# Output product of the last six half blocks with seven products for eight, and attention chunks every two steps

## The chip, the cores and the metric

The kernel runs on one core of a Trainium2 chip. The metric is the device time of an execution in microseconds. Each number quoted as a time is the median of four to eleven executions. A span, from the first to the last instruction in a trace, is some 2 us less than the time of the same execution. Times in the text that have a start, such as 346.78, are us from the start of the span. TensorE is PE in the profile, VectorE is DVE, ScalarE is ACT, GpSimd is POOL, and SyncE, which issues most transfers, is SP.

## The reference

Linear attention with a decaying state feeds a two-layer network with the activation h - tanh(h). All is float32.

```python
batch, n_heads, seq, head_dim = (4, 8, 768, 64)
n_tokens, d_model, d_ff = (3072, 512, 2048)

for t in range(S):                       # attention, per batch and head
    state = gamma[None, :, None, None] * state + einsum('bhd,bhe->bhde', k[:, :, t], v[:, :, t])
    y[:, :, t] = scale * einsum('bhd,bhde->bhe', q[:, :, t], state)
x = y.transpose(0, 2, 1, 3).reshape(B * S, H * D)
h = x @ w_in                             # 3072 x 512 by 512 x 2048
g = h - np.tanh(h)
return g @ w_out                         # 3072 x 2048 by 2048 x 512
```

## The kernel before

The 3072 tokens are 12 half blocks of 256 tokens. One step takes one half block and 256 of the 2048 hidden columns: an up product (x by w_in into PSUM), the activation on ACT and VectorE, and, two steps later, a down product (g by w_out). There are 96 steps. Attention is computed in chunks of 128 tokens, which are laid between the steps, from step 9 on one chunk in three steps.

The down product of a step is eight blocks of 128x128 by 256 columns, issued as four matmuls of 512 columns:

```python
    def down(n, m2, j, first, last):
        if first:
            o_p[j] = bank("o", f"o_{n}_{m2}_{j}")
            keep_busy(o_p[j][:, :P])
        for i in range(2):
            nc.tensor.matmul(o_p[j], gT[n, m2][:, i, ts(j, P)], w2[:, 2 * m2 + i],
                             start=(first and i == 0), stop=(last and i == 1))
```

The scores of a chunk need its q and k with head dimension on the partitions. From chunk 8 on that is done by two transfers: ACT splits the words into halves, a write takes them to memory (`rows`), and a transposing read brings them back (`kqT`). `products` has two groups of matmuls, and only the second needs `kqT`:

```python
    def turn_by_dma(ci):
        apart = mid.tile([P, 2, 2, H * D], U16, tag="apart", bufs=1)   # cut
        for which in range(2):
            words = loaded[ci][which].rearrange("p h d -> p (h d)").bitcast(U16)
            nc.scalar.copy(out=apart[:, :, which],
                           in_=words.rearrange("p (n two) -> p two n", two=2))
        rows = dram.tile([P, 2, 2 * H * D], U16, tag="rows")           # cut
        nc.sync.dma_start(out=rows, in_=apart.rearrange("p two i n -> p two (i n)"))
        sides[ci] = mid.tile([P, 2, NP, P], F32, tag="kqT")            # cut
        nc.sync.dma_start_transpose(out=sides[ci]..., in_=rows...)     # cut

    def products(ci):
        kh, _, vh = loaded[ci]
        kT, qT = (sides[ci][:, i] for i in range(2))
        ...                       # cut: k by v, 32 records, no kqT needed
        ...                       # cut: kT by qT, 32 records, need kqT
```

The loop over the steps. The order in which it names the operations is the order of every engine's queue. `turn_by_dma` stands at the end of a step, behind the activation in ACT's queue; what it makes for chunk ci + 3 is used by `products` at the start of the next chunk's step:

```python
    with_chunk = {BEGUN + 3 * i + 1: FIRST - 3 + i for i in range(NCH - FIRST + 3)}
    ...
    for s in range(BEGUN, len(steps)):
        n, m2, first, last = steps[s]
        ci = with_chunk.get(s)
        if ci is not None:
            if ci + 3 < NCH:
                scale(ci + 3, 0, nc.gpsimd)
                scale(ci + 3, 1, nc.gpsimd)
            if ci >= FIRST:
                outputs_rest(ci)
                keep_x(ci)
            if FIRST <= ci + 2 < NCH:
                products(ci + 2)
                mask(ci + 2)
                state(ci + 2)
            load_chunk(ci + 4)
            if FIRST <= ci + 1 < NCH - 1:
                outputs(ci + 1)
                see(ci + 1)
        for i in with_weights.get(s, []):
            convert(i)
            load_weights(i + 3)
        for i in range(2):
            up(n, m2, i)
        ...                                   # cut
        shrink_begin(n, m2)                   # two ACT operations
        shrink_factors(n, m2)                 # three ACT operations
        shrink_multiply(n, m2)
        downs(LAG)                            # the down product of two steps ago
        shrink_end(n, m2)
        if ci is not None and ci + 3 < NCH:
            turn_by_dma(ci + 3)
```

## Time and profile before

| | before |
|---|---|
| time | 752.49 us (752.43 to 754.41) |
| span of the trace (of an execution of 753.87 us) | 752.1 us |
| TensorE busy | 99% |
| a plain step (up and down) | 6.88 us |
| a chunk of attention, added to a step | 2.24 us |
| waits of TensorE for a transpose | none |

The views and how they are read are in the prediction below. A line of a group or of the timeline has the source line, engine, operation, and output<-inputs. In the chain of waits a line is start, duration, engine, tile, source line and number of records. Each float32 matmul of the source makes two records.

### The profile page before, as it was taken

The page shows a single profiled execution, that of the slowest core. Times are in us where ns is not written, and L with a number is a line of the kernel's source. Part 1 is how long each engine was busy: PE and PEld are TensorE (multiplying, and loading weights), DVE is VectorE, ACT ScalarE, POOL GpSimd, SP SyncE. Part 2 cuts the span into 40 slices and gives each one's busy share as a digit, 9 for nine tenths or more (in the row PEclk, how much of TensorE's full clock was granted, in tenths as well). Part 3 has the DMA queues.
Part 4 walks back from the last instruction along what each step waited for, and adds up shares of the span by engine and source line. Part 5 has one row for each costly group of instructions (what it writes and reads, how often), then busy time and mean ns, then how long its engine had stood idle before and what let it go on. Part 6 is the DMA issues. An engine that isn't in the chain of part 4 may idle for free.

```text
span 752.1 us, 13885 instructions
## 1 busy us (share of the span) xinstructions
PE 740.9 (99%) x5502; PEld 509.9 (68%) x5502; DVE 518.0 (69%) x807; ACT 389.4 (52%) x727; POOL 126.9 (17%) x108
## 2 busy tenths in 40 slices
PE   8899999999999999999999999999999999999997
PEld 7786667666767676766676676666666666666775
DVE  4889989998898666656565656565665666656653
ACT  4567576667665546445545545444344434434442
POOL 0565445445444111100111100000000000000000
PEclk9999999999999999999999999999999999999999
DMA  9972436556553353343342421000000000000000
GB/s 196 234 182 74 127 89 172 158 158 153 156 128 84 99 155 107 67 96 93 91 99 71 98 58 56 29 1 1 29 0 1 28 1 0 29 0 1 28 2 28
DMA packets 125680, 59.76 MB, mean 79 GB/s; under 512 B 109872, under 2 KB 118576, under 8 KB 125616
## 3 DMA queue, kind: packets, MB, share of 16 engines
q1 hardware_dynamic: 125328, 58.67, 29.9%
q8 instruction: 43, 0.70, 0.4%
q10 hardware_dynamic: 288, 0.21, 0.1%
q14 instruction: 21, 0.17, 0.1%
HBM read 35.80 MB, written 14.68 MB: 67 GB/s over the span
## 4 chain that ended last, share of the span: by engine, by line
PE 96%; DMA 2%; DVE 1%; SPq 1%; ACT 0%; issue 0%; ACTq 0%; DVEq 0%
PE h L414 44%; PE o L462 42%; PE y L352 3%; PE o L470 2%; PE s L298 2%; PE s L304 1%; PE kqTp L212 1%; PE kqTp L250 1%; DMA raw<-in_moe_w_in_dram 1%; DMA k<-in_k_dram 1%; SPq L229 1%; DMA out_dram<-sum 0%; SPq L154 0%; DVE power L187 0%; DVE head L185 0%; DVE a L311 0%
## 5 line engine op out<-in xcount | busy, mean ns | idle before, releaser
L414 PE MATMUL h<-xT,w 128*128 128x256 f32 x1536 | 349.9, 381 | 0.0
L414 PEld LDWEIGHTS h<-xT,w 128*128 128x128 f32 x1536 | 289.7, 190 | 68.4 <-issue 31.8
L462 PE MATMUL o<-w,g 128*128 128x512 f32 x736 | 331.9, 593 | 0.0
L462 PEld LDWEIGHTS o<-w,g 128*128 128x128 f32 x736 | 139.4, 190 | 135.1 <-issue 128.4
L423 ACT ACTIVATE u<-h 128x512 f32<-128x512 f32 x96 | 57.3, 597 | 289.0 <-PE h L414 288.9
L439 DVE TENSOR_TENSOR th<-h,th 128x512 f32<-128x512 f32 x96 | 66.3, 690 | 176.0 <-ACT th L424 176.0
L453 DVE COPY_PREDICATED g<-large,th 128x512 f32<-128x512 int32 x96 | 71.8, 748 | 10.2 <-DVE g L452 0.5
L442 DVE SCALAR_TENSOR_TENSOR h<-q,h 128x512 f32<-128x512 f32 x96 | 66.8, 696 | 10.4 <-DVE h L440 0.5
L448 DVE SCALAR_TENSOR_TENSOR h<-q,h 128x512 f32<-128x512 f32 x96 | 66.6, 694 | 8.2
L431 ACT ACTIVATE q<-u,tab 128x512 f32<-128x512 f32 x96 | 69.4, 722 | 0.0
L432 ACT ACTIVATE q<-u,tab 128x512 f32<-128x512 f32 x96 | 69.1, 720 | 0.0
L433 ACT ACTIVATE large<-u,tab 128x512 f32<-128x512 f32 x96 | 68.8, 717 | 0.0
L452 DVE TENSOR_TENSOR g<-h,u 128x512 f32<-128x512 f32 x96 | 66.3, 691 | 3.3
L440 DVE SCALAR_TENSOR_TENSOR h<-u,h 128x512 f32<-128x512 f32 x96 | 65.8, 685 | 0.0
L236 POOL TENSOR_TENSOR q<-q,tab 128x512 f32<-128x512 f32 x22 | 24.3, 1104 | 198.4 <-DMA q<-in_q_dram 115.1
L424 ACT ACTIVATE th<-h 128x512 f32<-128x512 f32 x96 | 56.9, 592 | 0.0
L195 POOL TENSOR_TENSOR low<-low,power 128x512 f32<-128x512 f32 x30 | 38.5, 1282 | 103.1 <-DVE power L187 89.1
L199 POOL TENSOR_TENSOR w<-low,head 128x512 f32<-128x512 f32 x30 | 38.7, 1289 | 2.4
L352 PEld LDWEIGHTS y<-a,v 64*64 64x64 f32 x768 | 15.8, 134 | 16.7 <-ACT large L433 10.6
L236 POOL TENSOR_TENSOR v<-v,tab 128x512 f32<-128x512 f32 x22 | 26.5, 1207 | 0.1
L382 ACT COPY seen<-y 64x1 f32<-64x1 f32 x96 | 10.1, 153 | 28.2 <-PE y L352 27.8
L393 ACT COPY xT<-y 128x512 f32<-128x512 f32 x24 | 14.1, 587 | 17.0 <-PE y L352 17.0
(54 smaller groups left out, 412.8 us busy)
## 6 DMA issues: line engine op xcount, KB each, us to landing
rows<-apart SPq DMA_DIRECT2D x16, 512.0 KB, 2.8
k<-in_k_dram SPq DMA_DIRECT2D x24, 256.0 KB, 4.3
q<-in_q_dram SPq DMA_DIRECT2D x24, 256.0 KB, 4.9
v<-in_v_dram SPq DMA_DIRECT2D x24, 256.0 KB, 5.1
raw<-in_moe_w_out_dram SPq DMA_DIRECT2D x12, 512.0 KB, 3.6
out_dram<-sum SPq DMA_DIRECT2D x23, 256.0 KB, 2.1
raw<-in_moe_w_in_dram SPq DMA_DIRECT2D x14, 256.0 KB, 4.2
raw<-in_moe_w_in_dram SPq DMA_DIRECT2D x28, 128.0 KB, 3.9
```

Of the source, the lines that this page charges most:

```text
L414: nc.tensor.matmul(hp, w1[:, c, ts(2 * m2 + i, P)], xT[n // 2][:, c, ts(n % 2, TH)], start=(i == 0 and c == 0), stop=(c == NC - 1), skip_g ...
L423: nc.scalar.activation(u, hp, AF.Square)
L431: nc.scalar.activation(q0, u, AF.Square, bias=bias0)
L432: nc.scalar.activation(q1, u, AF.Square, bias=bias1, scale=math.sqrt(A))
L433: nc.scalar.activation(large, u, AF.Relu, bias=bias_m)
L439: nc.vector.tensor_tensor(th, hp, th, op=ALU.subtract)
L440: nc.vector.scalar_tensor_tensor(hp, in0=u, scalar=R, in1=hp, op0=ALU.subtract, op1=ALU.mult, reverse0=True)
L442: nc.vector.scalar_tensor_tensor(hp, in0=q0, scalar=C0, in1=hp, op0=ALU.add, op1=ALU.mult)
L448: nc.vector.scalar_tensor_tensor(hp, in0=q1, scalar=A * C1, in1=hp, op0=ALU.add, op1=ALU.mult)
L452: nc.vector.tensor_tensor(flat, hp, u, op=ALU.mult)
L453: nc.vector.copy_predicated(flat, large.bitcast(I32), th)
L462: nc.tensor.matmul(o_p[j], gT[n, m2][:, i, ts(j, P)], w2[:, 2 * m2 + i], start=(first and i == 0), stop=(last and i == 1))
```

## The change

The intent is to save one matmul in eight of the down product. Two blocks of tokens by two blocks of hidden columns are multiplied with two by two blocks of w_out by Strassen's algorithm (in a form with shared sums): seven products with sums of the left blocks on POOL in every step, sums of the weights made once on POOL, and seven sums of the results on VectorE at the end of each half block. That needs the buffers of the weights' conversion and of the chunks' q and k, and all PSUM banks that attention uses. So it can be done only when attention is over. For that the chunks are put in one step of two; attention then ends in step 45, and the last six half blocks (steps 48 to 95) run with seven products. Third, x holds the even tokens of a half block first, and the output rows are stored to match.

```diff
+        half = xT[n][:, :, ts(nj // 2, TH)].rearrange("p (n r) t -> p r n t", r=2)
+        y = y_banks[:, ci % 2][:, :: 1 - 2 * (ci % 2)]
+        for odd in range(2):
+            nc.scalar.copy(out=half[:, :, :, ds(P * odd + D * (nj % 2), D)],
+                           in_=y[:, :, :, odd::2])
...
+    def fast_sums(n, m2):
+        g = gT[n, m2]
+        a11, a12, a21, a22 = (g[:, i, ts(j, P)] for j in range(2) for i in range(2))
+        s_ = inp.tile([P, 4, P], F32, tag="kq"[m2 % 2], name=f"s_{n}_{m2}", bufs=2)
+        s1, s2, s3, s4 = (s_[:, i] for i in range(4))
+        nc.gpsimd.tensor_tensor(s1, a21, a22, op=ALU.add)
+        nc.gpsimd.tensor_tensor(s2, s1, a11, op=ALU.subtract)
+        nc.gpsimd.tensor_tensor(s3, a11, a21, op=ALU.subtract)
+        nc.gpsimd.tensor_tensor(s4, a12, s2, op=ALU.subtract)
+        fast_g[n, m2] = (a11, a12, s4, a22, s1, s2, s3)
...
+        five, sixth = spare
+        first, second, third = five[:3]
+        acc = {1: first, 2: first, 5: second, 7: second, 3: third, 4: third, 6: sixth}
...
+        for k in (1, 6, 5, 7, 4, 2, 3):
+            right = (
+                w2[:, 2 * m2, :TH], w2[:, 2 * m2 + 1, :TH], w2[:, 2 * m2 + 1, TH:],
+                *(t_of[x, m2 // 2][:, m2 % 2] for x in (3, 0, 1, 2)),
+            )[k - 1]
+            nc.tensor.matmul(accs[n][k], left[k - 1], right, start=first and k in (1, 6, 5, 4),
+                             stop=last, skip_group_check=True)
...
+        nc.scalar.copy(out=p1, in_=acc[1])
+        for dst, k, b, how in (
+            (v_, 6, p1, add), (x_, 5, v_, add), (w_, 7, v_, add), (c22, 5, w_, add),
+            (c21, 4, w_, sub), (c11, 2, p1, add), (c12, 3, x_, add),
+        ):                                    # one VectorE operation each
...
-    with_chunk = {BEGUN + 3 * i + 1: FIRST - 3 + i for i in range(NCH - FIRST + 3)}
+    with_chunk = {BEGUN + 2 * i + 1: FIRST - 3 + i for i in range(NCH - FIRST + 3)}
...
+        if n >= FAST:                         # FAST = 6
+            fast_sums(n, m2)
+        if s in with_fast:
+            fast_weights(*with_fast[s])
         if ci is not None and ci + 3 < NCH:
             turn_by_dma(ci + 3)
```

More of the change, by code (lines that the diff above doesn't have):

```diff
@@ L392, in keep_x @@
             xT[n] = xp.tile([P, NP, BLK * P], F32, tag="xT", name=f"xT_{n}")
-        nc.scalar.copy(
-            out=xT[n][:, :, ts(nj, P)].rearrange("p (n r) t -> p r n t", r=2),
-            in_=y_banks[:, ci % 2][:, :: 1 - 2 * (ci % 2)],
-        )
+        half = xT[n][:, :, ts(nj // 2, TH)].rearrange("p (n r) t -> p r n t", r=2)
[3 more added lines that the diff above has]
+                           in_=y[:, :, :, odd::2])
     gT = {}
@@ L463, in down @@
                              start=(first and i == 0), stop=(last and i == 1))
-    def down_half(n, m2, j, c, first, last):
-        if first and c == 0:
-            o_p[j] = banks("t", f"o_{n}_{m2}_{j}")
-        for i in range(2):
-            nc.tensor.matmul(o_p[j][:, c, :TH], gT[n, m2][:, i, ts(j, P)],
-                             w2[:, 2 * m2 + i, ts(c, TH)],
-                             start=(first and i == 0), stop=(last and i == 1))
-    def store_half(n, j, c):
-        o = sums[n][0][:, j]
-        at = out[ds(n * TH + j * P, P)]
-        if c == 0:
-            nc.scalar.copy(out=o[:, :TH], in_=o_p[j][:, c, :TH])
-            nc.sync.dma_start(out=at[:, :TH], in_=o[:, :TH])
-            return
-        for quarter, copy, queue in (
-            (2, nc.vector.tensor_copy, nc.sync),
-            (3, nc.scalar.copy, nc.scalar),
-        ):
-            cols = ts(quarter, P)
-            copy(out=o[:, cols], in_=o_p[j][:, c, ts(quarter - 2, P)])
-            queue.dma_start(out=at[:, cols], in_=o[:, cols])
     def add_up(n, m2, j):
@@ L501, in add_up, with rows_of @@
         if done:
-            nc.sync.dma_start(out=out[ds(n * TH + j * P, P)], in_=o)
+            nc.sync.dma_start(out=rows_of(n)[:, j], in_=o)
+    def rows_of(n):
+        return out[ds(n * TH, TH)].rearrange("(p two) c -> p two c", two=2)
     runs = []
@@ L516, with quarter, fast_weights @@
     steps = [(n, m2, i == 0, i == len(r) - 1) for r in runs for i, (n, m2) in enumerate(r)]
+    FAST = 6
+    PAIRS = NM // 2
+    room = []
+    t_of = {}
+    def quarter(i, c, at):
+        return w2[:, i::2, ts(c, TH)][:, ds(2 * at, 2)]
+    def fast_weights(k, at):
+        if not room:
+            for _ in range(3):
+                raw = stage.tile([P, 2, 2, TH], F32, tag="raw", name="fast_raw", bufs=3)
+                room.extend(raw[:, i] for i in range(2))
+            for tag in ("head", "low", "power"):
+                room.extend(stage.tile([P, 2, TH], F32, tag=tag, name=f"fast_{tag}")
+                            for _ in range(2))
+            late = xp.tile([P, 4, 2, TH], F32, tag="xT", name="fast_x")
+            room.extend(late[:, i] for i in range(4))
+        t = t_of[k, at] = room[PAIRS // 2 * k + at]
+        a, b = (
+            (quarter(0, 1, at), quarter(0, 0, at)),
+            (quarter(1, 1, at), t_of.get((0, at))),
+            (quarter(1, 1, at), quarter(0, 1, at)),
+            (t_of.get((1, at)), quarter(1, 0, at)),
+        )[k]
+        nc.gpsimd.tensor_tensor(t, a, b, op=ALU.subtract)
@@ new lines @@
+    fast_g = {}
+    def fast_sums(n, m2):
[8 more added lines that the diff above has]
+        fast_g[n, m2] = (a11, a12, s4, a22, s1, s2, s3)
@@ new lines, with fast_banks @@
+    spare = []
+    accs = {}
+    def fast_banks(n):
+        if not spare:
+            t = banks("t", "fast_t")
+            whole = y_banks.rearrange("p two r n t -> p r two n t")
+            spare.append([t[:, 0], t[:, 1], whole[:, 0].rearrange("p two n t -> p (two n t)"),
+                          bank("o", "fast_o"), bank("o", "fast_o")])
+            spare.append(whole[:, 1].rearrange("p two n t -> p (two n t)"))
+        five, sixth = spare
+        first, second, third = five[:3]
+        spare[0] = five[3:] + [first, second, third]
+        acc = {1: first, 2: first, 5: second, 7: second, 3: third, 4: third, 6: sixth}
+        right = {2: 1, 7: 1, 4: 1, 6: n % 2}
+        accs[n] = {k: b[:, ts(right.get(k, 0), TH)] for k, b in acc.items()}
@@ new lines, in fast_down @@
+    def fast_down(n, m2, first, last):
+        if first:
+            fast_banks(n)
+        left = fast_g.pop((n, m2))
+        for k in (1, 6, 5, 7, 4, 2, 3):
[5 more added lines that the diff above has]
+                             stop=last, skip_group_check=True)
@@ new lines, in fast_end @@
+    def fast_end(n):
+        acc = accs.pop(n)
+        o = op.tile([P, 2, DM], F32, tag="sum", name=f"sum_{n}")
+        c11, c12, c21, c22 = (o[:, j, ts(c, TH)] for j in range(2) for c in range(2))
+        some = [mid.tile([P, 2, TH], F32, tag="a", name=f"fast_{n}") for _ in range(2)]
+        p1, v_, x_, w_ = (t[:, i] for t in some for i in range(2))
+        nc.scalar.copy(out=p1, in_=acc[1])
+        add, sub = ALU.add, ALU.subtract
+        for dst, k, b, how in (
+            (v_, 6, p1, add), (x_, 5, v_, add), (w_, 7, v_, add), (c22, 5, w_, add),
+            (c21, 4, w_, sub), (c11, 2, p1, add), (c12, 3, x_, add),
+        ):
+            if how is sub:
+                nc.vector.tensor_tensor(dst, b, acc[k], op=sub)
+            else:
+                nc.vector.tensor_tensor(dst, acc[k], b, op=add)
+            if k == 4:
+                nc.sync.dma_start(out=rows_of(n)[:, 1], in_=o[:, 1])
+        nc.sync.dma_start(out=rows_of(n)[:, 0], in_=o[:, 0])
@@ L518 @@
     waiting = []
     def part(j, n, m2, first, last):
-        if n == 2 * NB - 1 and j == 1:
-            for c in range(2):
-                down_half(n, m2, j, c, first, last)
-                if last:
-                    store_half(n, j, c)
-            return
         down(n, m2, j, first, last)
@@ L533, in downs @@
             tile_ = waiting.pop(0)
+            if tile_[0] >= FAST:
+                fast_down(*tile_)
+                if tile_[3]:
+                    fast_end(tile_[0])
+                continue
             for j in range(2):
@@ L597 @@
         with_weights[i - 5] = [i]
+    with_fast = {4 * NM // 2 + 1 + i: (i % 4, i // 4) for i in range(2 * PAIRS)}
     for s in range(BEGUN, len(steps)):
```

## The prediction

> **What bounds the kernel now.** I read the page from the top: the busy shares and slices, then the chain that ended last.
>
> ```profile
> PE 740.9 (99%) x5502; PEld 509.9 (68%) x5502; DVE 518.0 (69%) x807; ACT 389.4 (52%) x727; POOL 126.9 (17%) x108
> PE   8899999999999999999999999999999999999997
> PE 96%; DMA 2%; DVE 1%; SPq 1%; ACT 0%; issue 0%; ACTq 0%; DVEq 0%
> ```
>
> TensorE is busy in every slice and is 96% of the chain. The time is a sum of matmuls, so a matmul less should be time less, as long as nothing makes TensorE wait. The groups, one kind of matmul each, say where that time sits:
>
> ```profile
> L414 PE MATMUL h<-xT,w 128*128 128x256 f32 x1536 | 349.9, 381 | 0.0
> L462 PE MATMUL o<-w,g 128*128 128x512 f32 x736 | 331.9, 593 | 0.0
> L423 ACT ACTIVATE u<-h 128x512 f32<-128x512 f32 x96 | 57.3, 597 | 289.0 <-PE h L414 288.9
> ```
>
> L414 is the first product (x by w_in), L462 the output product, the one that the change touches. Each float32 matmul of the source appears as two records: a step has 8 in the source on L414, and 1536 records are 16 for each of 96 steps. The means (381, 593 ns) overlap; what counts is the pace in the chain. ACT waits 289 us for L414: it follows TensorE.
>
> The chain in order of time, around one chunk of attention (a 128-token piece, now one in three steps), gives the pace:
>
> ```profile
> 422.26 0.39 PE y L352 x16
> 422.65 0.47 PE s L298 x32
> 423.12 0.47 PE s L304 x32
> 423.58 0.70 PE y L352 x47
> 424.28 3.65 PE h L414 x16
> 427.94 3.43 PE o L462 x8
> 431.37 3.45 PE h L414 x16
> 434.82 3.43 PE o L462 x8
> 438.25 3.45 PE h L414 x16
> 441.71 3.43 PE o L462 x8
> 445.14 0.39 PE y L352 x16
> ```
>
> A plain step is 3.45 + 3.43 = 6.88 us. Chunk to chunk is 445.14 - 422.26 = 22.88 us, so a chunk adds 22.88 - 3 x 6.88 = 2.24 us. There are no gaps.
>
> Lastly, the timeline around the step of another chunk, for what must happen between two chunks. A chunk's q and k are split into halves by ACT, written to memory (rows), and read back transposed (kqT); L304 of the next chunk needs kqT:
>
> ```profile
> 308.75 0.65 PE L304 MATMUL s<-kqT 64*64 64x64 f32 x32
> 313.79 0.60 ACT L423 ACTIVATE u<-h 128x512 f32<-128x512 f32 x1 [3.18 <-PE h L414]
> 316.60 1.04 ACT L273 COPY apart<-k 128x1024 uint16<-128x1024 uint16 x1
> 317.53 1.05 ACT L273 COPY apart<-q 128x1024 uint16<-128x1024 uint16 x1
> 318.60 0.36 SPq L276 DMA_DIRECT2D rows<-apart  x1
> 321.30 1.85 SPq L278 DMA_TRANSPOSE kqT<-rows  x1
> 331.64 0.65 PE L304 MATMUL s<-kqT 64*64 64x64 f32 x32
> ```
>
> The table of DMA issues has the last link:
>
> ```profile
> kqT<-rows SPq DMA_TRANSPOSE x16, 4.2
> ```
>
> The reader should see a loop: L304 of a chunk at 308.75, this step's up product, five ACT operations, two copies, a write, a transpose issued at 321.30 that lands 4.2 to 4.4 us later, at about 325.6. The next L304 is at 331.64: 6 us of slack, in a schedule of three steps per chunk.
>
> **What the Trainium skill says.** (1) "TensorE: Matmul & The Clock Gate", Step-by-step, says that weight loads are pulled ahead of matmuls in flight. The trace agrees for exactly the shape that the change uses: L414 has a new load of 190 ns for every 256-column record and still runs 16 in 3.45 us, 216 ns each. (2) "DMA: Bandwidth & Descriptors", Anatomy of one DMA, puts about 2 us on any transfer, mostly completion; its Rules section says that a DMA which reads what another wrote waits for the first one's completion before it is issued. The trace agrees: the rows landed 2.6 us after their issue, and the transpose was issued 0.1 us after that. The two latencies stand in series and don't shrink when chunks come closer. (3) "GPSIMD Engine Reference", Elementwise, has a two-input float32 operation at 1.96 times VectorE's time. Here such operations took 1040 to 1290 ns against 690, 1.5 to 1.9 times. (4) The TensorE page, clock gate, says that the clock falls after an idle window of about 3.4 us; the trace is at 0.998 and shows no such idle, so only a wait that long would matter.
>
> **The change, part by part.**
>
> *Seven products for eight.* A step's output product is 8 blocks of 128x128 by 256 columns. In blocks of 256 columns (L414, and L470 in the last half block at 8 records in 1.73 us) one costs 3.45/8 = 0.431 us. Seven cost 3.02 us against 3.43: 0.41 to 0.42 us a step. Six half blocks of 8 steps are 48 steps; I count 47 here, 0.42 x 47 = **-19.7 us**, and the last in the end below. Each of the seven has its own weights, a load of 190 ns beside 431, hidden as in L414.
>
> *Sums for the left side*, four of 128x128 a step on POOL. From 1.04 to 1.29 us for 512 columns I estimate 0.35 to 0.5 us each, at most 2 us a step, on an engine with nothing else by then. g is ready some 5.6 us after its up product ends (L453 of the last step ends at 743.3, that product's records at 737.7), and is used two output and two up products later, 2 x 3.02 + 2 x 3.45 = 12.9 us. Hidden, +0.
>
> *Weight sums*, 16 on POOL of some 1.2 us, in steps 33 to 48, before first use in step 50. Hidden.
>
> *Recombination*, seven VectorE operations of 128x256 on PSUM; the same shape took 0.41 to 0.43 us (L323, L327), so 2.9 us per half block in place of one copy of 0.69 on VectorE and one on ACT. VectorE's own work is six operations of about 0.7 us, 4.2 us of a 6.5 us step, so it catches up in the next step; the five rotating banks give an up product (3.45 us) of room. Hidden, +0.
>
> *The end.* Before, from the last output products (744.40) to the end (752.1) 7.7 us, with a 0.86 us wait inside. After: 3.02 of matmuls, perhaps 0.3 for the last POOL sums, about 0.9 for the last two VectorE operations, 2.1 for the store (its row's median), 1.0 as before from landing to the end: 7.3. About **-0.4 us**.
>
> *x in two copies*, half the size each (a 128x256 ACT copy took 0.37 us against 0.59 for 128x512): +0.15 us of ACT in its idle time. +0.
>
> *A chunk every two steps.* TensorE, VectorE and ACT do the same chunk work, only sooner, so by busy shares it costs nothing. But the loop above gets only 2 x 6.88 + 2.24 = 16.0 us. From the start of L304 to the landing of the next kqT, over all 15 pairs in the trace, the loop takes 16.6 to 17.35 us, mean 16.9 (the one shown: 325.6 - 308.75 = 16.85), plus 0.1 to start. The mean natural distance, (468.70 - 126.86)/15 - 6.88 = 15.9. So TensorE, which works in order, should stand at L304 for about 1.1 us in each of 15 chunks: 16 us. It is a true loop: the next u, copies and transpose start from where TensorE resumes, so the wait comes back each time. The first transposed chunk is worse: its transpose was issued at 119.41 and landed 4.3 us later at 123.7, while its L304, at 126.86 now, comes one step earlier, near 119.9: 3.8 us. Together **+20 us**, and with fewer collisions, at 0.8 us a chunk, +16.
>
> Sum: 752.5 - 19.7 - 0.4 + 16 to 20 = 748.4 to 752.4. I take **750 us**: the matmuls saved in the second half are spent waiting in the first.
>
> **The rivals.** *A: the loop fits and nobody waits.* Then 752.5 - 20.1 = 732 us, 2.7% faster. For it speaks that TensorE is 99% busy and DMA engines are half idle; against it, 15 of 15 loops are longer than 16.0 us. Faster by over 2% needs 737.4 or less, a wait of under 5 us in all, where I count 16 at the least. *B: the denser DMA stretches the loop further.* In steps 9 to 26 chunk loads, rows, transposes and weights share the queues, and rows took up to 3.9 us and transposes 4.6 there. One more microsecond in nine loops makes 759 us. Against it: SP issues in order, so chunk loads and transposes stay apart. *C: VectorE becomes the bound in those steps.* It is at 9 tenths in the early slices (six operations, weight conversion and sums come to nearly a step). But a chunk brings it about 1.5 us (0.68 + 0.41 + 0.42) and TensorE 2.24, so denser chunks don't raise the ratio; it would add a few microseconds. *D: POOL or the recombination holds the fast half.* If the sums took twice my estimate they would still fit the 12.9 us; a stall at each of six half blocks of 1 us would be 6 us.
>
> **Range and chances.** Savings are firm to 1 us, since every duration was measured in the same shape. The wait is 0.6 to 1.5 us in 15 loops plus 2 to 4 once, 11 to 26 us. That gives 743 to 759; I take **742 to 758**. Faster by over 2% needs rival A almost whole: 0.07. Slower by over 2% (767.5) needs B and D together: 0.03. Within 2%: 0.90.
>
> **What would show it.** In the changed trace: output steps of the last six half blocks at 3.02 us and pairs of steps at 6.47; a TensorE wait for the kqT transpose, missing before, in about 16 places of some 1 us, the first near 4; chunk to chunk 17.0 us and not 16.0; no wait for POOL or VectorE of note in the second half; attention ending some 104 us sooner (its last step is 45 and not 63: 18 steps of 6.88 us are 124, less the 20 of waits). The prediction is wrong if chunk to chunk is 16.0, if the transposes land sooner than 4.1 us, or if TensorE stands in the fast half.

## The result

The changed kernel takes 758.68 us (758.23 to 759.18, four runs) against 752.49 us. The ratio is 1.0077, with a 95% interval of 1.0062 to 1.0092: no gain and 0.8% slower. A ratio is taken over the fast runs of both kernels, and is not quite the ratio of the medians that are quoted.

The page of the changed kernel, busy shares and the chain by engine:

```profile
PE 726.8 (96%) x5758; PEld 560.8 (74%) x5758; DVE 532.0 (70%) x843; ACT 389.4 (51%) x749; POOL 230.8 (30%) x316
PE 70%; DMA 14%; DVE 6%; ACT 6%; issue 2%; SPq 1%; POOL 0%; DVEq 0%; ACTq 0%; POOLq 0%
```

TensorE has 14 us less to do, and only 70% of the chain is TensorE, which was 96%. DMA is now 14% of it. Who TensorE waited for stands in the view of waits (total us, times, longest):

```profile
PE s L308 <- DMA kqT<-rows: 16.7, 16, 3.5
```

That line did not exist before. The chain in order of time, from one chunk's score products to the next, shows the loop; where a "..." stands, the short pieces between are left out:

```profile
346.78 0.69 PE s L308 x32
...
348.17 3.67 PE h L420 x16
...
354.16 0.61 ACT large L439
354.77 1.89 ACT apart L277 x2
...
356.68 2.63 DMA rows<-apart
...
359.37 4.10 DMA kqT<-rows
...
363.51 0.69 PE s L308 x32
```

The chain now runs through up product, activation, copies, write and transpose back to the score products, and the down product (beside the activation) and the whole second step are not on it. From 346.78 to 363.51 it takes 16.73 us.

In the fast half the same view shows a step as planned. Seven products of 0.43 us stand between two up products, 452.74 - 446.26 = 6.48 us a step against 6.88, without a gap:

```profile
446.26 3.45 PE h L420 x16
449.72 0.43 PE fast_t L579 x2
...
452.74 3.45 PE h L420 x16
```

Two more things stand out. The first wait, in TensorE's timeline, with the idle time before an instruction in brackets:

```profile
119.43 0.69 PE L302 MATMUL s<-v,k 64*64 64x64 f32 x32
123.58 0.87 PE L308 MATMUL s<-kqT 64*64 64x64 f32 x32 [3.46 <-DMA kqT<-rows]
124.38 5.18 PE L420 MATMUL h<-xT,w 128*128 128x256 f32 x16
```

The up product behind it takes 5.11 us in the chain where 3.45 is normal. The view by stretches shows the clock. A line has the stretch, its length, the busy time of PE, PEld, DVE, ACT and POOL, and then the clock that TensorE was granted:

```profile
120.54:123.95 3.41, 0.37 (x24) 0.37 (x28) 3.14 (x5) 0.00 (x0) 3.33 (x3) 1.00 0.95 215
123.95:127.36 3.41, 3.41 (x31) 2.75 (x22) 3.24 (x7) 0.00 (x0) 1.67 (x2) 0.50 1.18 220
```

TensorE was busy for 0.37 us of the first 3.41, and then had half the clock for 3.41 us. That is a loss of 1.7 us, as much as the up product was late; from 127.36 us on the view has 1.00 again.

And the end, in the timeline of all engines:

```profile
750.30 0.59 PE L579 MATMUL y<-w,s 128*128 128x256 f32 x2
750.50 0.37 ACT L588 COPY fast<-fast_t 128x256 f32<-128x256 f32 x1 [6.38 <-PE fast_t L579]
751.00 0.42 DVE L597 TENSOR_TENSOR fast<-y,fast 128x256 f32<-128x256 f32 x1 [4.15 <-PE y L579]
...
753.26 0.41 DVE L597 TENSOR_TENSOR sum<-y,fast 128x256 f32<-128x256 f32 x1
```

All seven recombining operations run after the last matmul (750.30 + 0.59), one after another, to 753.67.

Where the time went, from the two traces. A wait is counted as the start of L308 less the start of L302, less the 0.47 us (0.52 in the first two chunks) that lies between them undisturbed; this includes the tail of the products ahead, which the idle time in brackets does not.

| stretch | before | changed | difference |
|---|---|---|---|
| start to the up product of step 6 | 85.09 | 85.07 | 0.0 |
| from there to the last up product (734.23, 737.72) | 649.14 | 652.65 | +3.5 |
| of which 45 steps of 6.885 now 6.477 | | | -18.4 |
| of which 16 waits for transposes: 3.6, 2.3, and fourteen of 0.7 to 1.3 | | | +19.6 |
| of which the slow up product, 5.11 and not 3.45 | | | +1.7 |
| of which left over | | | +0.6 |
| from the start of the last up product to the end | 17.87 | 18.98 | +1.1 |
| span | 752.1 | 756.7 | +4.6 |

The times differ by 6.2 and these spans by 4.6. The traced execution of the kernel before was a long one (753.87 us): in seven later executions its span was 750.8 us in the median (749.8 to 751.2), which is 1.3 us of it; the other 0.3 lies outside the spans. The first row is the same work in nearly all kernels here, and yet takes from 83.8 to 85.4 us in their thirteen traces. So up to 1.6 us between two executions can come from the start, and what follows goes by stretches of the traces more than by spans.

### The profile page after: what moved, and what is told of

Read it like the earlier page. It is cut to its first block, busy times and chain, and to the rows that moved or that the text cites. A ratio compares the mean times of both kernels' runs of the same rounds, so it can differ in the third digit from the quotient of the medians.

```text
span 756.7 us, 14749 instructions
## 1 busy us (share of the span) xinstructions
PE 726.8 (96%) x5758; PEld 560.8 (74%) x5758; DVE 532.0 (70%) x843; ACT 389.4 (51%) x749; POOL 230.8 (30%) x316
## 4 chain that ended last, share of the span: by engine, by line
PE 70%; DMA 14%; DVE 6%; ACT 6%; issue 2%; SPq 1%; POOL 0%; DVEq 0%; ACTq 0%; POOLq 0%
PE h L420 37%; PE o L468 9%; DMA kqT<-rows 8%; PE fast_t L579 7%; PE y L579 6%; PE fast_o L579 5%; DMA rows<-apart 5%; ACT apart L277 3%; PE y L356 2%; PE s L308 2%; ACT q L437 1%; ACT q L438 1%; ACT large L439 1%; ACT th L430 1%; PE kqTp L254 1%
## 5 line engine op out<-in xcount | busy, mean ns | idle before, releaser
L468 PE MATMUL o<-w,g 128*128 128x512 f32 x384 | 173.0, 593 | 0.0
L468 PEld LDWEIGHTS o<-w,g 128*128 128x128 f32 x384 | 72.6, 190 | 71.4 <-issue 68.4
L544 POOL TENSOR_TENSOR s<-g 128x128 f32<-128x128 f32 x48 | 21.9, 455 | 294.4 <-DVE g L459 214.1
L459 DVE COPY_PREDICATED g<-large,th 128x512 f32<-128x512 int32 x96 | 73.9, 770 | 9.5
L308 PE MATMUL s<-kqT 64*64 64x64 f32 x768 | 16.5, 223 | 16.7 <-DMA kqT<-rows 16.7
L579 PE MATMUL fast_t<-w,g 128*128 128x256 f32 x96 | 28.6, 380 | 0.0
```

Of the source, the lines that this page charges most:

```text
L459: nc.vector.copy_predicated(flat, large.bitcast(I32), th)
L579: nc.tensor.matmul(accs[n][k], left[k - 1], right, start=first and k in (1, 6, 5, 4), stop=last, skip_group_check=True)
```

## The experiments

My theory: the wait for the transposes (19.6 us) and what it does to the clock (1.7 us) eat the saving, because the loop from one chunk's scores to the next chunk's is longer than two steps and a chunk. The rivals: the seven products and their sums cost more than counted; denser transfers or VectorE hold TensorE; the wait is long for another reason than the loop. All kernels gave correct results.

**e1_two_steps: one part of the change alone.** In the kernel before:

```diff
-    with_chunk = {BEGUN + 3 * i + 1: ...
+    with_chunk = {BEGUN + 2 * i + 1: ...
```

> The kernel before with one edit: a chunk every two steps, eight products as they were. Theory (the loop from one chunk's score products to the landing of the next transpose is longer than two steps and a chunk): TensorE stands about 19 to 20 us at the score products, the first time 3.6 us with a slow-clock product after it (1.7 us), so about 752.5 + 21 = 773 us. Rival (the missing time belongs to the seven products or their sums, and the spacing costs nothing): 752 us.

Measured: 775.69 us against 752.57, ratio 1.0314 (1.0296 to 1.0331). The waits, counted as above, are 4.1, 2.2 and then 0.7 to 1.3 us, 19.6 us in all, and the up product behind the first took 5.34 us. The spacing alone, with no Strassen in the kernel, costs 23 us. The first rival falls.

**e2_turn_early: shorten the loop, leave everything else.** In the changed kernel:

```diff
         for i in with_weights.get(s, []):
             convert(i)
-            load_weights(i + 3)
+        if ci is not None and ci + 3 < NCH:
+            turn_by_dma(ci + 3)
+        for i in with_weights.get(s, []):
+            load_weights(i + 3)
         for i in range(2):
             up(n, m2, i)
 ...
-        if ci is not None and ci + 3 < NCH:
-            turn_by_dma(ci + 3)
     downs(0)
```

> The changed kernel with one edit: the transpose of the next chunk (two ACT copies, a write, a transposing read) is issued ahead of the step's up product and not at the end of the step, so that it no longer waits for the five ACT operations behind that product. Theory: the loop gets 3 to 5 us shorter, from about 16.9 to 12 to 14 us, under the 16.0 that two steps and a chunk give; the 16 waits (19.6 us) and the slow-clock product (1.7 us) go, 758.7 - 21.3 = about 737 us. Rival (DMA contention of denser chunks, or VectorE, holds TensorE): the waits stay, or move to another operand, and the time stays above 750.

Measured: 737.76 us against 752.57, ratio 0.9806 (0.9791 to 0.9820). So 20.9 us are gained on the changed kernel's 758.68. In its timeline of SP and ACT the copies start right behind the chunk:

```profile
296.63 0.65 PE L308 MATMUL s<-kqT 64*64 64x64 f32 x32
...
298.33 1.04 ACT L277 COPY apart<-k 128x1024 uint16<-128x1024 uint16 x1
...
304.04 1.88 SPq L282 DMA_TRANSPOSE kqT<-rows  x1
...
312.46 0.65 PE L308 MATMUL s<-kqT 64*64 64x64 f32 x32
```

The transpose is issued 7.4 us after L308 starts, where the chain of the changed kernel had 359.37 - 346.78 = 12.6. From L308 to L308 it is 15.83 us here and 16.04 to 16.07 between most chunks, no more than two steps and a chunk take. Counted as in the prediction, from the start of L308 to the landing of the next transpose, the loop is 12.4 us in the mean of 15 pairs, where the kernel before has 16.9. Chunks are as dense as in the changed kernel and the same bytes move, and the waits are gone but for 0.7 and 0.3 us in the first two chunks. The writes even took longer (3.6 us in the median against 2.6, at most 5.9), and nobody waited for them. So neither contention nor VectorE held TensorE.

**e3_before_turn_early: control.** The same edit in the kernel before, where chunks are three steps apart.

> Control: the same early transpose in the kernel before, with a chunk every three steps. Theory: there the loop had 6 us to spare, nothing waits for it, so 752 us, no change within 1 us. Rival (the early place is a gain of its own, by another route): several us faster.

Measured: 752.66 against 752.57 us, ratio 1.0006 (0.9991 to 1.0021). The early place is no gain of its own. It pays only where the loop is what ends last.

**e4_fast8_three: seven products without the denser chunks.** In the changed kernel:

```diff
-    FAST = 6
+    FAST = 8
 ...
-    with_chunk = {BEGUN + 2 * i + 1: ...
+    with_chunk = {BEGUN + 3 * i + 1: ...
```

> The changed kernel with the chunks back at one in three steps, which leaves room for seven products in the last four half blocks only (32 steps). Theory: no waits for transposes; 29 steps of 0.41 us saved before the last up product (-11.9), the end 1.1 us longer than before: about 741.7 us. Rival (the seven products themselves cost more than was counted, in waits for POOL or VectorE): 747 or more.

Measured: 743.39 against 752.57 us, ratio 0.9879 (0.9862 to 0.9896), 1.7 us over what was expected. In the trace no TensorE wait for a transpose is left. From the up product of step 6 to the last one it takes 638.00 us, 11.1 less than before, where 29 x 0.408 = 11.8 were to be saved. The missing 0.7 us is taken up under e7_even; the other 1.0 us does not lie in this stretch and stays open.

**e6_fill: the clock.** In the changed kernel, between the two groups of score products:

```diff
+        if ci == 8:
+            idle[0] = 14
+            keep_busy(sp[:, 0, :P])
```

> The changed kernel with 14 dummy products of 128x128 on TensorE in the first and longest wait (3.5 us) for a transpose, which is not made shorter. Theory: the up product behind that wait took 5.11 us in place of 3.45 because the clock had fallen in the idle time; kept busy, it takes 3.6, and the time is 758.7 - 1.6 = about 757.1 us. Rival (it was slow for another reason, such as operands that came late): it stays at 5.1 us and the time at 758.7.

Measured: 756.34 against 752.50 us, ratio 1.0052 (1.0040 to 1.0064), where the changed kernel had 1.0077. TensorE's timeline:

```profile
123.02 0.70 PE L311 MATMUL s<-kqT 64*64 64x64 f32 x32 [0.67 <-DMA kqT<-rows]
123.65 3.72 PE L423 MATMUL h<-xT,w 128*128 128x256 f32 x16
```

The transpose lands as late as before, but the up product behind it takes its normal time: from L308 (here L311) to the down product 4.2 us and not 5.8. By stretches its granted clock is 1.00 from 120 to 130 us. Idle time cost more than its length: the operands were the same, only TensorE had been kept busy. The times alone would not show it: of the 2.3 us between the two medians, the traces have 1.1 in the start, ahead of the fill.

**e9_middle: a smaller dose.** The changed kernel with `turn_by_dma(ci + 3)` between `shrink_begin` and `shrink_factors`, three ACT operations earlier.

> A smaller dose of the early transpose: in the changed kernel the copies for it stand between the first two and the last three of the step's five ACT operations, so the loop is shorter by three ACT operations at the pace of 0.61 to 0.72 us, about 1.9 us. Theory (a loop whose excess over 16.0 us is waited out): the waits of 0.7 to 1.3 us in the later chunks go altogether, the first one (3.6 us) falls to 1.8 and the second (2.3) to 0.4, and the clock does not fall; 19.6 - 2.2 + 1.7 = 19.1 us gained, about 739.6 us. Rival (only the place ahead of the up product helps, because the transposes collide with other transfers): little gained, over 750 us.

Measured: 742.56 against 752.83 us, ratio 0.9859 (0.9844 to 0.9873). Fifteen of the sixteen waits are gone but for 0.3 us in one of them, as a cut of 1.9 us from an excess of about 1 us should do: the loop is 15.2 us in the mean, and at the one chunk with 0.3 us left 16.3. But the first wait did not shrink: 3.5 us idle, and a slow up product (4.63 us) behind it; that is most of the 4.8 us to e2_turn_early. My expectation for it was wrong. The trace has the reason: ACT had its second copy done at 111.07, but the write was issued at 114.34, because three weight loads stood ahead of it in SP's queue, issued from 112.57 on. In e2_turn_early the write was placed ahead of these loads, and the wait fell to 0.7 us. So the first wait hung on the order of SP's queue, the others on ACT's. For the first wait that is read from the two traces; no run changed SP's order alone.

**e10_copy_twice: the other direction.** The changed kernel with the copy of k made twice:

```diff
-        for which in range(2):
+        for which in (0, 0, 1):
```

> The other direction: in the changed kernel the ACT copy of k ahead of each transpose is made twice, which lengthens the loop by one copy, 0.94 us at its pace. ACT is some 51% busy, so by busy shares this costs nothing. Theory: every one of the 16 waits grows by that much, 758.7 + 15 = about 774 us. Rival (the wait has slack in it, or the loop is not closed): 759 to 762 us.

Measured: 778.30 against 752.83 us (772.59 to 780.96), ratio 1.0346 (1.0321 to 1.0370). In the trace TensorE's idle time before these products grows from 16.7 to 30.0 us over the same 16 waits, 0.83 us each for a copy of 0.94, and the up products behind the first two waits (3.3 and 3.2 us) are both slow (5.21 and 4.94 us). An ACT operation of 1 us, on an engine that is half idle, costs TensorE nearly that much in each chunk. The traced execution (span 770.5) was the shortest of four; the others, up to 778.8, show a granted clock of 0.987 to 0.990 against its 0.992. So the clock fell more often in them, but over their spans that accounts for at most 1.6 to 4.0 of the 5.0 to 8.3 us that they are longer. The rest is not traced, and neither is why the median is 4 us over what was expected.

**e7_even: the third part of the change alone.** The kernel before with even tokens first in x and the output rows to match.

> The kernel before with the even tokens first in x and the rows of the output to match (two ACT copies of half the size per chunk, stores of 2 KB rows with a stride), nothing else. Theory: ACT has idle time ahead of every up product, so no change: 752.5 us within 1. Rival (the third part of the change costs some of the 6 us): 753.5 to 758.

Measured: 753.84 against 752.50 us, ratio 1.0017 (1.0004 to 1.0030). It is small, but not nothing: from the up product of step 6 to the last one the trace has 649.99 us and not 649.14, and chunks are 22.94 us apart and not 22.88. In that trace the 0.06 us lies in the output products of a chunk (0.76 us in the chain and not 0.70). It is about the size of the 0.7 missing in e4_fast8_three, where these products take 0.76 us too. In the changed kernel's chain they take 0.70, so this does not explain the +0.6 that was left over in the table above. Why it costs anything stays open.

**e5_order: the end.** In the changed kernel:

```diff
-        for k in (1, 6, 5, 7, 4, 2, 3):
+        for k in (1, 2, 6, 5, 7, 4, 3):
```

> The changed kernel with the seven products in the order 1, 2, 6, 5, 7, 4, 3 in place of 1, 6, 5, 7, 4, 2, 3. Theory: at the end the copy of product 1 waited until product 2, in the same PSUM bank, was done, so that all seven VectorE operations came after the last matmul; and product 6 waited 0.5 us for its POOL sum. With 2 second, the copy and four of the operations run beside the matmuls: the end 2 to 2.6 us shorter, 758.7 - 2.5 = about 756.2 us, nothing else moved. Rival (the operations wait for all of the step's matmuls whatever the order): under 0.5 us gained.

Measured: 756.83 against 752.50 us, ratio 1.0063 (1.0046 to 1.0079). The end, from the start of the last up product, went from 18.98 to 18.55 us, nearly all of it TensorE's shorter wait for a POOL sum. The copy of product 1 did start earlier, but the first VectorE operation still waited for the last matmul. The rival was nearer, and my account of the end had to be amended: product 6, which that operation reads, and product 3 lie in different banks of one tile.

**e8_best: early transpose and new order.**

> Early transpose and new order of products together on the changed kernel. Theory: the two are independent, 737.8 - 2.5 = about 735.3 us, over 2% faster than the kernel before. Rival (the end is hidden behind something else once the waits are gone): 737 to 738.

Measured: 736.95 against 752.50 us, ratio 0.9791 (0.9778 to 0.9804). Against e2_turn_early the order gains 0.8 us and not 2.5, as e5_order would say.

**e11_tiles: the end again.** On e8_best:

```diff
+        if n == 2 * NB - 1:
+            third = five[4]
 ...
-        for k in (1, 2, 6, 5, 7, 4, 3):
+        for k in (1, 2, 5, 7, 6, 4, 3):
```

> e8_best with two edits for the end: the order is 1, 2, 5, 7, 6, 4, 3, and in the last half block products 4 and 3 go to a PSUM bank of a tile of its own and not of the tile that holds product 6. In e5_order the copy of product 1 began when product 7, in the other bank of the same tile, was done, and the first VectorE operation when product 3, in the tile of product 6, was done. Theory (an operation waits for the last matmul into the tile that it reads, not into its bank): now the copy follows product 7 and the first sum follows product 6, so that they start beside the last matmuls; the first VectorE operation begins before the last matmul ends, and the time from the last up product's start to the end falls from 18.5 to about 17.6 us; about 736 us. Rival (they wait for the end of the step's matmuls whatever the tile): 18.5 us as before.

Measured: 735.22 against 752.45 us, ratio 0.9771 (0.9758 to 0.9784). In the timeline of the end the first sum now begins before the last matmul does:

```profile
727.62 0.42 DVE L599 TENSOR_TENSOR fast<-y,fast 128x256 f32<-128x256 f32 x1 [2.84 <-PE y L581]
727.78 0.59 PE L581 MATMUL fast_o<-w,s 128*128 128x256 f32 x2
```

The end takes 733.3 - 715.64 = 17.7 us, as expected. In these traces an operation waits for the last matmul into the tile that it reads, whatever the bank. This is the fastest kernel, 2.3% faster than the kernel before.

## Why the prediction was right or wrong

The mechanism was right, and the size was off: 750 us with a range to 758 was told, and 758.68 was measured. The steps that failed are three terms of the sum. The end was told 1.2 us shorter and became 1.1 us longer, a miss of 2.3 us and the largest; the fall of the clock, 1.7 us, had no term; and the waits were taken at 18 us and came to 19.6.

- *The loop.* Right. It was told that TensorE would stand for the transpose in about 16 places, near 4 us the first time and about 1 us after it, 16 to 20 us in all. It was 3.6, then 0.7 to 1.3 (2.3 in the second chunk, which has less attention work ahead of it), 19.6 us in all. I took 18 of it in the sum; +1.6. From the second chunk on, chunk to chunk is 16.5 to 17.3 us where 17.0 was told. That it is a closed loop is shown from both sides: e2_turn_early and e9_middle take the excess away, e10_copy_twice adds to it. The kernel before had 6 us to spare at the same place by its trace, and a shorter loop gained it nothing (e3_before_turn_early).
- *Seven products.* Right. A step is 6.48 us where 6.47 was told. The saving is 0.408 us for 45 steps to the last up product where I took 0.42, +0.5 us. The sums on POOL took 0.455 us each, within the 0.35 to 0.5 estimated, and hide, except in the last step.
- *The clock.* This was the step that I had in hand and did not take. The prediction says that "only a wait that long would matter" of about 3.4 us, and foresees a wait of 3.8 us some lines on, but puts no time for it in the sum. It cost +1.7 us (e6_fill, and the granted clock of 0.50 for 3.41 us). The reading behind it was wrong too. The trace before does show such a fall: from 32.09 to 35.51 us, in the start, its granted clock is 0.50, after an idle time of 2.94 us. The mean of 0.998 is this stretch, and a mean hides it.
- *The end.* Mis-sized. "About -0.4 us" beside the saving in the two steps before it means 1.2 us less from the last up product on; it became 1.1 us more, a miss of 2.3. I took two VectorE operations to be left after the last matmul. There were seven, from 751.00 to 753.67 us, because the operations waited for a tile and not for a bank (e5_order, e11_tiles); and the last step waited 0.5 us for POOL.
- *x in two copies.* "+0" was 0.85 us in the trace of e7_even and 1.3 in its time. In the changed kernel 0.6 us are left over, and whether this is their cause is not shown.
- *Rivals.* A (nobody waits) was wrong for this kernel; with the loop opened the kernel reaches 737.76 us, and with the end mended too 735.22, where A had 732. B (contention stretches the loop) did not happen: a write took 2.6 us in the median and a transpose 4.2, where the kernel before had 2.8 and 4.2. C and D did not happen, but for the end.
- *What is left.* The misses, 1.6 + 0.5 + 1.7 + 2.3 and a last one of 0.6 to 1.3, make 6.7 to 7.4 of the 8.3 us between 750.4 (the sum with 18 us of waits) and 758.7. The rest is about the 1.3 us by which the traced execution of the kernel before was longer than the usual one. The start varies by that much between traces, but the usual executions were not traced, so where it lies is not shown.

## What to carry to other kernels

When work that goes through memory and back is packed more densely, busy shares say nothing about its cost: follow one round of it from use to use, add the latencies, and hold the sum against the new distance. A loop with 6 us to spare leaves no mark on the busy shares or on the chain that ended last, and becomes the bound once the distance falls below it; the cheap remedy is to issue its first link earlier in each queue that it passes, ACT's and SP's here. A mean clock near 1 does not say that no wait cost clock: look at the clock by stretches around each wait. At the end of a kernel, look at which tile, not only which bank, the last sums wait for.

## What the Trainium skill lacked or had wrong

- "TensorE: Matmul & The Clock Gate", Part 1, puts the fall of the clock after an idle window of about 3.4 us (the table at its end speaks of gaps over about 3 us). Here the low clock did come in stretches of 3.41 us, but idle times of 3.46, 3.95 and also of 3.2 us (e10_copy_twice) were followed by an up product of 4.9 to 5.3 us and not 3.45, and in the kernel before 2.94 us in the start were enough. After 2.1 us it took 3.67, as behind the other chunks. After 3.5 us in e9_middle it was 4.63: the half clock had begun at 122.19, 1.4 us ahead of it. What the page lacks is how little work counts as idle. The thirteen traces have 16 falls ahead of the last matmul; in the 3.41 us before each, TensorE was busy for 0.25 to 1.72 us. Among the other stretches on the same grid of 3.41 us, the least busy had 1.57. So the bound lies near half by these traces; no run was made to find it.
- "DMA: Bandwidth & Descriptors", Latency and other measured facts, gives an effective bandwidth of 261 GB/s for a transposing transfer with a middle dimension that is not contiguous, but for a transpose no time from issue to landing, which is what a loop pays. Here 512 KB took 4.1 to 4.6 us, after a write of the same 512 KB of 2.6 us or more: 6.8 us for the way out and back.
- No page that I read says that an operation may wait for all matmuls into a tile that spans two PSUM banks. Here it put seven operations behind the last matmul, and giving the last products a tile of their own took the end from 18.5 to 17.7 us.
